# Causal masks added by VectorE and a two-part values operand in the last two batches of an attention and mixer kernel

## Chip, cores and metric

One NeuronCore of a Trainium2 chip. The metric is the device time of one execution in microseconds (us); the kernel before took 888.46 us (median of 3 runs, 887.33 to 892.19). All data are float32.

## What is computed

The kernel chains three layers over 4 batches of 448 rows and 768 channels. The change lies in the first, causal attention with 12 heads of 64 channels:

```python
scores = scale * np.matmul(q, k.transpose(0, 1, 3, 2))
mask = np.triu(np.ones((seq, seq), dtype=bool), k=1)
scores = np.where(mask, -1000000000.0, scores)
scores = scores - np.max(scores, axis=-1, keepdims=True)
attn = np.exp(scores)
attn = attn / (np.sum(attn, axis=-1, keepdims=True) + 1e-09)
return np.matmul(attn, v)
```

A token and channel mixer follows (`u = x + (relu(xt @ w_tok1) @ w_tok2)` transposed back, then `u + relu(u @ w_ch1) @ w_ch2`), and a gated layer with a spatial product and an output projection.

## The kernel before

**Tiling.** Two heads are a pair; there are 6 pairs a batch and 24 in all, numbered n = 0 to 23. A pair's 448 queries are four chunks, `CHUNKS` (line 25): number 0 has 64 queries, 1, 2 and 3 have 128 each. Chunk i sees only the keys up to its own end, so it is 64, 192, 320 or 448 columns wide; j is the head within the pair.

**Two ways to multiply.** Pairs 0 to 11 (the first two batches, `whole`, line 279) give float32 operands to TensorE as they are. Pairs 12 to 23 split each operand into a high part that float32r holds and the low rest, and use three products of parts (high by high, high by low, low by high). From pair 12 on a pair has only one buffer of each kind (`side`, `before`, lines 160 to 166).

**A pair's steps** (`pair_jobs`, line 275):
- `lq`, `lv`: loads of queries, keys and values on the SP queue; `qs` scales the queries on GpSimd (POOL). For pairs 12 to 23 `qh`, `ql`, `kl`, `vh`, `vl` make the parts, on ScalarE (ACT) and POOL.
- `SA`, `SB` (line 334): the scores of chunks 3 and 0, and of 2 and 1, on TensorE (PE). Behind each chunk's products (line 351) come matmuls that add the mask: a selecting matrix `eye` by a triangle `tri` of -1e9 (line 359), two of them for chunk 0 and four for each other chunk, so 14 a pair.
- `M` (line 371): VectorE (DVE) finds the negated maximum of both heads of a chunk at once, out of PSUM. `E` (line 378): ACT takes the exponential out of PSUM into the tiles `pbig` and `psml` and accumulates the sums. `R` (line 382): DVE inverts the sums. `Pn` (line 393): POOL multiplies the eight exponentials of a pair by them.
- `T0`, `Ta`, `Tb` (line 402): PE transposes the blocks; ACT copies them out (`H`), and for pairs 12 to 23 DVE makes the low parts (`L`).
- `PV0`, `PVa`, `PVb` (lines 435 to 463): PE multiplies values by transposed blocks into one PSUM bank (`v`), one head in the upper and one in the lower 64 rows. For pairs 12 to 23 each product is three matmuls (lines 440 to 442), 21 a pair.
- `UE`: ACT copies the result into `U`. `UT`, `XH`, `XL`: PE turns it back, ACT and DVE make parts for the token mixer.

**The rest in the same list.** `group_jobs` does the token mixer after every third pair. `weight_jobs` changes 24 channel-mixer weights from pairs of words to float32 in three DVE steps (lines 104, 106, 108) and two POOL steps (lines 71, 77), and stores them to DRAM. `channel_jobs` loads them again (`wb`) for each batch and does the channel mixer: 24 blocks of 18 matmuls a batch (lines 119 to 121, tile `cps`). The last layer stands behind the list, written in order.

**The order.** All these steps are jobs with an engine, a planned cost, predecessors, a rank and perhaps a PSUM bank or buffer. `emit` (line 214) takes, again and again, the ready job that can start earliest by its plan, and of several the one of lowest rank; ranks are the pair or block number plus an offset from the table `RK` (line 260). That fixes the order of each engine's instructions; an engine whose next instruction isn't ready waits, whatever stands behind it. Pairs 12 to 23 are thus mixed with the channel mixer of earlier batches, which fills PE.

## Time and profile before

| what | value |
|---|---|
| median of 3 runs | 888.46 us |
| profiled execution, its own time | 889.3 us |
| its span, first to last instruction | 887.5 us |
| busy: PE, DVE, ACT, POOL | 854.4, 432.8, 300.3, 293.5 us |
| mean granted TensorE clock | 0.988 of full speed |
| matmuls | 4768 |

A busy time is the sum over which an engine had at least one instruction running. Matmuls are pipelined: one row of PE overlaps the next, so what a matmul costs is the distance from its start to the next start, not its own duration. An engine's idle time before an instruction is put down to what released it.

### The profile page before, as it was taken

Reading aid. Unit: us, or ns where it says so; the run is one execution under the profiler, and the core shown is the slowest. Engines: PE = TensorE matmul, PEld = TensorE weight load, DVE = VectorE, ACT = ScalarE, POOL = GpSimd, SP = SyncE. Lnnn points to the kernel's source line nnn. Section 1 sums busy time; section 2 is a strip of 40 time slices with the busy share of each in tenths; the row PEclk is TensorE's granted clock in tenths of the full one; section 3 lists DMA queues with packets and bytes.
Section 4 is the critical chain, followed back from the end, with each engine's and each line's share of the span. In section 5 each row is a group of like instructions: output and inputs, shape, how many; then the busy total and the mean of one; then the engine's idle time right before and its main releaser. Section 6 shows DMA issues by size and latency. Waiting matters only on the chain.

```text
span 887.5 us, 12703 instructions
## 1 busy us (share of the span) xinstructions
PE 854.4 (96%) x4768; PEld 740.2 (83%) x4768; DVE 432.8 (49%) x775; ACT 300.3 (34%) x816; POOL 293.5 (33%) x378
## 2 busy tenths in 40 slices
PE   7898998788999999999999999999999999999998
PEld 5576766677789899998988899999999888889997
DVE  4795886885634533433443345511134543467441
ACT  5765564242223423333342301200013431433110
POOL 3588697774633223323233201200003200224000
PEclk9999999898999999999999999999999999999999
DMA  4676685876762555455344538876662200000112
GB/s 142 188 265 219 215 302 201 308 258 276 272 251 87 195 178 205 140 176 198 114 161 155 175 107 285 318 259 216 213 215 78 71 1 1 1 1 31 70 56 94
DMA packets 45613, 148.65 MB, mean 167 GB/s; under 512 B 17008, under 2 KB 21744, under 8 KB 45552
## 3 DMA queue, kind: packets, MB, share of 16 engines
q1 hardware_dynamic: 42096, 128.96, 43.0%
q10 hardware_dynamic: 3456, 18.88, 5.4%
q8 instruction: 38, 0.62, 0.3%
q14 instruction: 23, 0.19, 0.1%
HBM read 123.44 MB, written 24.38 MB: 167 GB/s over the span
## 4 chain that ended last, share of the span: by engine, by line
PE 83%; POOL 6%; DVE 4%; DMA 3%; ACT 2%; issue 2%; ACTq 0%; POOLq 0%; SPq 0%
PE cps L119 13%; PE cps L120 12%; PE cps L121 12%; PE pst L406 4%; PE sa L351 3%; PE pso L437 3%; PE psg L120 2%; PE psg L121 2%; PE psg L119 2%; PE pso L121 2%; PE pso L119 2%; PE pso L120 2%; PE psv L119 2%; PE psv L120 2%; PE psv L121 2%; POOL pbig L393 2%
## 5 line engine op out<-in xcount | busy, mean ns | idle before, releaser
L119 PE MATMUL cps<-uhl,wb 128*128 128x448 f32 x288 | 109.3, 380 | 3.8 <-DMA wb<-w 3.8
L119 PE MATMUL cps<-hid,wb 128*128 128x448 f32 x288 | 108.3, 376 | 2.3 <-DMA wb<-w 1.4
L120 PE MATMUL cps<-uhl,wb 128*128 128x448 f32 x288 | 106.3, 369 | 0.0
L121 PE MATMUL cps<-uhl,wb 128*128 128x448 f32 x288 | 106.1, 368 | 0.0
L121 PE MATMUL cps<-hid,wb 128*128 128x448 f32 x288 | 105.4, 366 | 0.0
L120 PE MATMUL cps<-hid,wb 128*128 128x448 f32 x288 | 105.3, 365 | 0.0
L393 POOL TENSOR_SCALAR pbig<-pbig,rcp 128x448 f32<-128x448 f32 (+1 forms) x96 | 65.1, 687 | 90.6 <-DVE rcp L384 85.3
L84 DVE SCALAR_TENSOR_TENSOR hid<-cps,hid 128x448 fp32r<-128x448 f32 x48 | 29.9, 623 | 108.8 <-ACT hid L702 108.8
L378 ACT ACTIVATE pbig<-sa,nm 128x448 f32<-128x448 f32 (+1 forms) x72 | 42.6, 597 | 105.4 <-DVE nm L371 59.6
L702 ACT ACTIVATE hid<-cps 128x448 fp32r<-128x448 f32 x48 | 26.1, 544 | 139.9 <-PE cps L121 139.9
L710 DVE TENSOR_TENSOR U<-cps,U 128x448 f32<-128x448 f32 x48 | 29.9, 624 | 81.4 <-PE cps L121 80.6
L77 POOL TENSOR_TENSOR winl<-win,winh 128x1536 fp32r<-128x1536 f32 x4 | 14.8, 3691 | 165.1 <-ACT winh L69 165.1
L371 DVE TENSOR_REDUCE nm<-sa 128x2 f32<-128x896 f32 (+1 forms) x72 | 46.2, 680 | 39.0 <-PE sa L359 38.6
L119 PEld LDWEIGHTS cps<-uhl,wb 128*128 128x128 f32 x288 | 54.8, 190 | 8.5 <-issue 4.1
L119 PEld LDWEIGHTS cps<-hid,wb 128*128 128x128 f32 x288 | 54.1, 188 | 8.0 <-DVE U L710 2.3
L121 PEld LDWEIGHTS cps<-uhl,wb 128*128 128x128 f32 x288 | 54.8, 190 | 4.6
L120 PEld LDWEIGHTS cps<-uhl,wb 128*128 128x128 f32 x288 | 55.0, 191 | 4.0
L121 PEld LDWEIGHTS cps<-hid,wb 128*128 128x128 f32 x288 | 54.1, 188 | 4.6
L120 PEld LDWEIGHTS cps<-hid,wb 128*128 128x128 f32 x288 | 54.2, 188 | 4.1
L406 PE MATMUL pst<-ident,pbig 128*128 128x128 f32 x288 | 48.3, 279 | 8.4 <-POOL pbig L393 8.2
L77 POOL TENSOR_TENSOR wn<-wn 128x768 fp32r<-128x768 f32 x24 | 46.3, 1928 | 1.6
L406 PEld LDWEIGHTS pst<-ident,pbig 128*128 128x128 f32 x288 | 35.0, 142 | 12.7 <-POOL pbig L393 11.2
(186 smaller groups left out, 1974.1 us busy)
## 6 DMA issues: line engine op xcount, KB each, us to landing
wb<-w SPq DMA_DIRECT2D x96, 768.0 KB, 4.3
dbl<-in_w SPq DMA_DIRECT2D x24, 768.0 KB, 5.7
w<-wn ACTq DMA_DIRECT2D x24, 768.0 KB, 5.3
stage<-in_qkv SPq DMA_DIRECT2D x24, 448.0 KB, 4.3
out_t<-out SPq DMA_DIRECT2D x24, 224.0 KB, 1.9
dbl<-in_winu SPq DMA_DIRECT2D x4, 768.0 KB, 5.8
dbl<-in_winv SPq DMA_DIRECT2D x4, 768.0 KB, 6.0
dbl<-in_wout SPq DMA_DIRECT2D x4, 768.0 KB, 4.3
```

The source lines that it names most:

```text
L77: e.tensor_tensor(lo, x, hi.bitcast(F32), op=ALU.subtract)
L84: nc.vector.scalar_tensor_tensor(lo, x, 0.0, hi.bitcast(F32), op0=ALU.max, op1=ALU.subtract)
L119: nc.tensor.matmul(ps, ah, bh, start=(first and i == 0), stop=False)
L120: nc.tensor.matmul(ps, ah, bl, start=False, stop=False)
L121: nc.tensor.matmul(ps, al, bh, start=False, stop=(last and i == n - 1))
L351: nc.tensor.matmul(out, x[rows, q0:q1], y[rows, S : 2 * S][:, ks[j]], start=(t == 0), stop=False, skip_group_check=True)
L371: nc.vector.tensor_reduce(nm[:M], S_.ps[:M, :, o : o + W], axis=mybir.AxisListType.X, op=ALU.max, negate=True)
L378: nc.scalar.activation(P(n, i)[:M, j, :], S_.ps[:M, j, o : o + W], AF.Exp, bias=SM[n, i][:M, j : j + 1], scale=1.0, accum_out=sums[n % 2][ ...
L393: nc.gpsimd.tensor_scalar(x, x, rcp[n % 2][:M, 2 * ((i - 1) % 4) + j :][:, 0:1], 1.0, op0=ALU.mult, op1=ALU.mult)
L406: nc.tensor.transpose(me.ps[:, o : o + M], src(), ident[:M, :M])
L437: nc.tensor.matmul(out, v32[e][:, k], m[0], start=first, stop=last, skip_group_check=True)
L710: nc.vector.tensor_tensor(U[b][:, d, :], first.ps, U[b][:, d, :], op=ALU.add)
```

## The change

- For pairs 12 to 23 the mask matmuls go. `make_mask` writes two mask tiles once, on POOL, before pair 12. In place of one maximum for both heads, `M` becomes one DVE instruction for each chunk and head, eight a pair: it adds the mask to the scores in PSUM, writes the negated sum into the exponential's own tile in SBUF, and keeps the least element, the negated maximum. `E` reads that tile in SBUF with scale -1 and no longer holds the PSUM bank.
- For pairs 12 to 23 the values' high and low parts stand side by side in one stationary operand of 128 columns for each chunk and head. Each product is two matmuls (by the high and the low part of the transposed block), so the product of the two low parts is included too. The two heads can't share a bank's rows now: each head has its own chain `PV0`, `PVa`, `PVb`, one after the other in the one bank `v`, 16 matmuls a pair. ACT copies one half of the rows into `U` and DVE adds the other half, for each head.
- Values of these pairs are loaded by one DMA instead of three; their parts are made by six POOL instructions instead of four.
- For pairs 0 to 11 the multiplication `Pn` of the narrow chunks 0 and 1 (four a pair) moves from POOL to ACT.
- The planned costs of several jobs, `NARROW` and nearly all offsets in `RK` change, and with them the order of instructions on all engines.

```diff
-NARROW = (980, 1150, 1160)
+NARROW = (840, 1300, 1280)
...
-                v = slot("G7", [2, VS], F32R, "v")
-                parts12[what] = [v[:, 0, :], v[:, 1, :]]
-                for t in parts12[what]:
-                    nc.gpsimd.memset(gaps(t).bitcast(F32), 0.0)
+                v = parts12[what] = slot("G7", [8, 2 * D], F32R, "v")
+                nc.gpsimd.memset(v[64:128, 0, :].bitcast(F32), 0.0)
+                nc.gpsimd.memset(v[0:64, 7, :].bitcast(F32), 0.0)
...
-    RK = dict(s=53.0, q=-0.3, v=14.0, e=26.8, pn=-68.2, f=43.8, hl=-6.2, pv=-11.9, ue=33.0, ut=-111.3, x=-99.8, h=59.1, hr=-23.0, u=59.0, uc=55.2, us=45.6, ld=-58.4, ch=71.8, hd=-31.0, ad=-6.0, nw=76.8, nh=72.7, wi=295.1)
+    RK = dict(s=74.7, q=-0.5, v=28.2, e=26.7, pn=-105.7, f=41.2, hl=-38.3, pv=-27.5, ue=29.5, ut=-154.8, x=-87.8, h=60.5, hr=-82.0, u=81.8, uc=64.9, us=61.3, ld=-6.8, ch=79.3, hd=-95.7, ad=-78.8, nw=69.0, nh=16.7, wi=310.3)
...
+        places = [(slice(0, 128), slice(1, 7), slice(1, 7)), (slice(0, 64), slice(0, 1), slice(0, 1)), (slice(64, 128), slice(0, 1), slice(7, 8))]
...
+        def make_mask(_):
+            masks12.extend(slot(tag, [S], F32, "mask") for tag in ("mask", "p1"))
+            for t, o in zip(masks12, (0, S - 128)):
+                nc.gpsimd.memset(t, 0.0)
+                diag = t[:, o : o + 128]
+                nc.gpsimd.affine_select(out=diag, in_=diag, compare_op=ALU.is_ge, fill=MASKED, base=0, pattern=[[-1, 128]], channel_multiplier=1)
+
+        if n == 2 * NP:
+            job(("mk",), "POOL", 1200, make_mask, after=[("T0", n - 1), ("Ta", n - 1, 0), ("Ta", n - 1, 1), ("SA", n - 1), ("SB", n - 1)], rank=r + RK["q"])
...
-                            nc.tensor.matmul(out, x[rows, q0:q1], y[rows, S : 2 * S][:, ks[j]], start=(t == 0), stop=False, skip_group_check=True)
+                            nc.tensor.matmul(out, x[rows, q0:q1], y[rows, S : 2 * S][:, ks[j]], start=(t == 0), stop=(t == 2), skip_group_check=True)
+                    if not whole:
+                        continue
...
+                    nc.vector.tensor_tensor_reduce(
+                        out=P(n, i)[:M, j, :],
+                        in0=S_.ps[:M, j, o : o + W],
+                        in1=masks12[0][:M, :W] if j == 0 or M == 64 else masks12[1][:M, S - W : S],
+                        scale=-1.0,
+                        scalar=3.0e38,
+                        op0=ALU.add,
+                        op1=ALU.min,
+                        accum_out=SM[n, i][:M, j : j + 1],
+                    )
...
+                    src = S_.ps[:M, j, o : o + W] if whole else P(n, i)[:M, j, :]
+                    nc.scalar.activation(P(n, i)[:M, j, :], src, AF.Exp, bias=SM[n, i][:M, j : j + 1], scale=1.0 if whole else -1.0, accum_out=acc)
...
+                    top_ = job(("M", n, i, j), "DVE", 150 + W / 0.96, low, after=[S_, *old, ("mk",)], rank=r + RK["e"]).uses(S_)
...
+                if whole and i < 2:
+                    nc.scalar.mul(x, x, f)
+                else:
+                    nc.gpsimd.tensor_scalar(x, x, f, 1.0, op0=ALU.mult, op1=ALU.mult)
...
+        def pvx_parts(j, V, blocks, dst, last):
+            def run(_):
+                for c, o in blocks:
+                    s0 = CHUNKS[c][0]
+                    for k in range(2):
+                        nc.tensor.matmul(V.ps[:, s0:S], split_tiles("v")[:, c + 3 * j], dst[k][:, o : o + S - s0], start=False, stop=(last and k == 1 and c == 3), skip_group_check=True)
...
+                W_ = job(("PV0", n), "PE", 420, pv0_parts(j), after=[("L", "T0", n), vfit] + [("PV0", n)] * j, rank=r + RK["pv"], bank="v")
...
+                def first_part(_, j=j, x=x, W_=W_):
+                    nc.scalar.copy(x, W_.ps[64 - 64 * j : 128 - 64 * j, :S])
+
+                def both_parts(_, j=j, x=x, W_=W_):
+                    nc.vector.tensor_tensor(x, W_.ps[64 * j : 64 * j + 64, :S], x, op=ALU.add)
```

## Rows read from the trace of the kernel before

**Rows 1.** Stretches of the span: each engine's busy us (instructions), granted clock, DMA share, GB/s.

```profile
0.00:153.50 153.50, 137.88 (x850) 98.26 (x851) 107.53 (x174) 90.47 (x297) 107.08 (x151) 0.98 0.67 221
153.50:245.50 92.00, 79.71 (x456) 66.77 (x454) 65.59 (x85) 28.80 (x85) 59.49 (x64) 0.93 0.76 274
245.50:515.00 269.50, 267.77 (x1683) 241.27 (x1684) 104.10 (x196) 96.80 (x275) 81.72 (x140) 1.00 0.49 167
515.00:700.00 185.00, 185.00 (x906) 169.55 (x905) 67.58 (x131) 33.54 (x59) 21.73 (x10) 1.00 0.61 210
```

**Rows 2.** Waits of PE in its first 250 us: us in total, times, longest.

```profile
PE pst L406 <- POOL pbig L393: 7.0, 7, 2.2
...
PE cps L119 <- DMA wb<-w: 5.1, 3, 3.8
```

**Rows 3.** Timeline of PE, mask matmuls (L359): start us, us, instruction.

```profile
382.99 0.33 PE L359 MATMUL sa<-cst 64*128 64x128 f32 x4
383.24 0.47 PE L119 MATMUL cps<-hid,wb 128*128 128x448 f32 x1
...
404.18 0.31 PE L359 MATMUL sa<-cst 64*128 64x128 f32 x4
404.32 0.34 PE L351 MATMUL sa<-qk 64*64 64x64 f32 x6
404.49 0.23 PE L359 MATMUL sa<-cst 64*64 64x64 f32 x2
404.65 0.47 PE L119 MATMUL cps<-hid,wb 128*128 128x448 f32 x1
```

**Rows 4.** Timeline of PE, values by transposed blocks of one pair.

```profile
395.12 0.36 PE L440 MATMUL pso<-T,v 128*128 128x448 f32 x1
...
395.73 0.34 PE L440 MATMUL pso<-Tab,v 128*64 128x384 f32 x1
...
396.26 0.28 PE L440 MATMUL pso<-Tab,v 128*64 128x256 f32 x1
...
396.61 0.22 PE L440 MATMUL pso<-Tab,v 128*64 128x128 f32 x1
...
396.79 0.39 PE L440 MATMUL pso<-Tab,v 128*128 128x384 f32 x1
...
397.77 0.27 PE L441 MATMUL pso<-Tab,v 128*128 128x128 f32 x1
397.88 0.27 PE L442 MATMUL pso<-Tab,v 128*128 128x128 f32 x1
398.00 0.42 PE L119 MATMUL cps<-hid,wb 128*128 128x448 f32 x1
398.25 0.36 PE L120 MATMUL cps<-hid,wb 128*128 128x448 f32 x1
```

**Rows 5.** Groups by line and shape on DVE and ACT: busy us, mean ns.

```profile
L710 DVE TENSOR_TENSOR U<-cps,U 128x448 f32<-128x448 f32 x48 | 29.9, 624 | 81.4 <-PE cps L121 80.6
...
L371 DVE TENSOR_REDUCE nm<-sa 128x2 f32<-128x896 f32 x24 | 26.0, 1083 | 24.1 <-PE sa L359 24.1
...
L378 ACT ACTIVATION_READ_ACCUMULATOR pbig<-sa,nm 128x1 f32 x72 | 14.3, 199 | 0.0
...
L464 ACT COPY U<-pso 128x448 f32<-128x448 f32 x24 | 12.8, 532 | 33.7 <-PE pso L442 26.1 <-PE pso L437 7.6
```

**Rows 6.** Groups on POOL, the multiplications Pn: wide chunks together, then narrow ones.

```profile
L393 POOL TENSOR_SCALAR pbig<-pbig,rcp 128x448 f32<-128x448 f32 (+1 forms) x96 | 65.1, 687 | 90.6 <-DVE rcp L384 85.3
...
L393 POOL TENSOR_SCALAR psml<-psml,rcp 128x192 f32<-128x192 f32 x48 | 24.7, 524 | 0.0
...
L393 POOL TENSOR_SCALAR psml<-psml,rcp 64x64 f32<-64x64 f32 x48 | 16.7, 360 | 0.0
```

**Rows 7.** Timeline of DVE, one step of the weights' change of format, twice.

```profile
143.19 0.55 DVE L104 TENSOR_SCALAR wn<-dbl 128x768 uint32<-128x768 uint32 x1
...
154.71 2.50 DVE L104 TENSOR_SCALAR wn<-dbl 128x768 uint32<-128x768 uint32 x1
```

More of the change, by code (lines that the diff above doesn't have):

```diff
@@ L435, in product @@
         def product(out, k, m, first=False, last=False):
[L436 to L442 removed]
+            nc.tensor.matmul(out, v32[e][:, k], m[0], start=first, stop=last, skip_group_check=True)
         def pv0(me):
@@ L458, in pvx, with pv0_parts, run @@
             return run
-        last = V
-        for j in range(2):
-            last = job(("PVa", n, j), "PE", 650 if whole else 3 * 174, pvx(j, [(1, 0)], da[j], False), after=[last, ("L", "Ta", n, j)], rank=r + RK["pv"]).uses(V)
-            last = job(("PVb", n, j), "PE", 680 if whole else 3 * (117 + 59 + 51 * j), pvx(j, [(2, 0), (3, 256)], db[j], j == 1), after=[last, ("L", "Tb", n, j)], rank=r + RK["pv"]).uses(V)
-        UE = job(("UE", n), "ACT", 540, lambda _: nc.scalar.copy(U[b][:, p, :], V.ps[:, :S]), after=[last], rank=r + RK["ue"]).uses(V)
+        def pv0_parts(j):
+            def run(me):
+                me.ps = psa.tile([128, 512], F32, tag=me.tile, name="pso")
+                for k in range(2):
+                    nc.tensor.matmul(me.ps[:, :S], split_tiles("v")[:, 7 * j], d0[k], start=(k == 0), stop=False, skip_group_check=True)
+            return run
```

94 lines of the change are left out of this document (56 added, 38 removed).

## The prediction

> **What bounds the kernel now.** First the table of stretches [rows 1], which divides the span by what TensorE (PE) waits for. From 245.5 to 515 us PE has an instruction running for 267.77 of 269.50 us, and from 515 to 700 us for all of 185.00; every other engine is below half of either stretch. There only less work for PE can shorten the kernel, and any such work counts in full. Ahead of that PE is idle for 15.6 us until 153.5 us and for 12.3 us until 245.5 us; in the second of these the mean granted clock is 0.93, so part of it ran at 1.2 GHz in place of 2.4. VectorE (DVE) and GpSimd (POOL) are at 71% and 65% there, ScalarE (ACT) at 31%. Then the waits of PE in its first 250 us [rows 2]: the longest sum, 7.0 us, is for POOL's multiplication of the exponentials, the next, 5.1 us, for channel weights that come back from DRAM. So this early part is bound by chains through all engines, not by one of them.
>
> Then the timeline of PE inside the dense part [rows 3, 4]. Matmuls overlap, so I read costs as distances between starts. The scores of pairs 12, 13 and 14 fall into the loose stretch up to 245.5 us, those of pairs 15 to 23 into the dense one.
>
> **Masks leave PE.** The four mask matmuls behind chunk 3 take 404.18 to 404.32, so 0.14 us; those behind chunk 2 sit in the same way between two score products, another 0.14; the two behind chunk 0 take 404.49 to 404.65, 0.16; the four behind chunk 1 take 382.99 to 383.24, 0.25 [rows 3]. Together 0.69 us a pair. The last two numbers contain the step from the half-height matmuls to the full-height ones of the channel mixer, which stays when the scores themselves come last. If all of that stays, only 0.28 us goes; if none, 0.69. I take 0.50, in the middle: two matmuls of 64 columns and four of 64 to 128 must be worth something. Over 12 pairs 6.0 us, bounds 3.4 and 8.3.
>
> The Trainium skill, TensorEngine Tiling (Array Packing), Key Properties, speaks against the middle value: a change of tiling mode (not of the tile) drains TensorE. By that rule the step out of a score block is a drain that stays, the gain is the 3.4 us of the lower bound, and the time below would be 881.6 in place of 879.0. The trace agrees so far that the step out takes 0.16 and 0.25 where a step inside takes 0.14; how much of it is the masks' own it doesn't show.
>
> **Values by blocks: 21 matmuls become 16.** The block of one pair runs from 395.12 to 398.00, 2.88 us [rows 4]. From starts three matmuls apart: 448 columns cost (395.73 - 395.12) / 3 = 0.203 us, 384 cost 0.177, 256 cost 0.117, 128 cost 0.06 behind a stationary operand of 64 columns and 0.11 behind one of 128 (397.77 to 397.88). Afterwards every operand has 128 columns, and for each head there are two of each width: 4 x (0.203 + 0.177 + 0.117 + 0.11) = 2.43 us, 0.45 less. The block now comes in two pieces, and leaving one costs 0.25 in place of 0.20 (398.00 to 398.25), so 0.40 a pair, 4.8 us in all. If the narrow ones stay at 0.06 it is 0.60 a pair, 7.2 us.
>
> **What takes the masks over.** DVE loses four maxima a pair, of both heads and 2048 columns together, and gains eight additions with a maximum over the same 2048 columns, plus two additions of 448 columns. The old maxima cost 1.083 us for 896 columns, so 2.5 us a pair; the nearest row for the new ones reads PSUM and SBUF and writes SBUF, 624 ns for 448 columns [rows 5]. Eight at that price would be 5.0 us, the same rate as the maxima 2.5; six of eight are narrower, so I take 3.2. With 2 x 0.624 for the second halves DVE has about 1.9 us more a pair, bounds 1.2 and 3.7. ACT gets one more copy, 0.532 us [rows 5]. In the dense part both are hidden: DVE is busy for 104.10 and ACT for 96.80 of 269.50 us [rows 1], and PE has channel blocks that need neither. If that cover went, the nine dense pairs would cost 9 x 1.9 = 17 us.
>
> In the loose stretch the cover is thin. DVE is busy for 65.59 of 92.00 us with the weights' change of format that PE waits for. Three pairs bring 5.7 us there; I let half reach PE, 2.8 us, bounds 0 and 5.7. The mask tiles cost POOL four instructions once; at 687 ns, the row of its wide multiplications [rows 6], at most 2.7 us. Pair 12's maxima now stand behind them and behind pair 11's transposes, and what is queued behind those maxima on DVE waits too: the format steps. I price it at nothing, since POOL and DVE have slack of 32.5 and 26.4 us in that stretch, and keep 2.7 as the bound.
>
> The Trainium skill, VectorE: DVE Perf Modes, Two Vector instructions with no wait between them, adds a price: an operation that also writes out its accumulator is two instructions. No row of before has one on DVE. ACT's separate read of an accumulator takes 199 ns [rows 5]; eight of that size would be an estimated 1.6 us a pair, or 4.8 us more for the three loose pairs, and with half of it on the path the time below would be 881.4.
>
> **The narrow multiplications.** In pairs 0 to 11 four of eight move from POOL to ACT. A pair's eight now cost POOL 4 x 0.687 + 2 x 0.524 + 2 x 0.360 = 4.5 us, of which 1.77 us move, 39% [rows 6]. Of PE's 7.0 us behind this line [rows 2] I count 39%, 2.7 us, as gained, bounds 0 and 7.0. ACT has room: 90.47 of 153.50 us [rows 1] and 12 x 1.77 = 21 us more at POOL's own prices.
>
> **Edits at no cost.** One load in place of three on the SP queue: fewer issues of the same bytes. The values' six part-making instructions in place of four on POOL: each extra one is at most the 0.360 us of a 64 x 64 multiplication [rows 6], and POOL is at 81.72 of 269.50 us. The exponential from SBUF: same columns. New ranks and planned costs: they move no work between engines; in the dense part any order that keeps PE supplied takes the same time, in the loose part it can go either way, which I put into the range with 5 us on both sides.
>
> **The sum.** Masks 6.0 and values 4.8 give 10.8 us less PE work. A quarter of it, 2.7 us, belongs to pairs 12 to 14 in the loose stretch; half of that is lost to waiting, leaving 9.4. The early gain of 2.7 and the early loss of 2.8 cancel. The profiled execution took 889.3 us, so 879.9; the median of the runs is 0.84 lower, so 879.0 us.
>
> **Rivals.**
> - *Early stretch tightens.* All 10.8 us count, 2.7 us of waits for POOL go, and half of the slow clock's price: 0.07 of 92 us is 6.4 us, so 3.2. That is 16.7 us, 871.8. For it: one format step on DVE takes 0.55 us with POOL idle and 2.50 us while POOL works [rows 7], so 21 us taken from POOL can speed DVE too. With the masks at their upper bound it reaches 869. Against it: the waits for channel weights stay.
> - *Early stretch eats the gain.* All 5.7 us of DVE work and the 2.7 us of mask tiles reach PE in place of the 2.8 I counted: 884.6. For it: the second stretch is already DVE's.
> - *Slower: the second head waits for the one bank.* Head 1's first product can start only when ACT (0.532 us) and DVE (0.624 us) [rows 5] have emptied head 0's bank. If the fixed order puts too little PE work between, PE stands for 1.16 us and everything behind it too: 12 x 1.16 = 13.9 us, 892.9. It loses more than the change gains from 0.8 us a pair on (9.4 / 12). Against it: the plan counts 540 and 620 for these two steps and so places other blocks between; for it: it doesn't know what else waits in ACT's and DVE's queues.
> - *The masks cost nothing where they are:* the 3.4 us above, 881.6, inside the forecast's own range.
>
> **How the numbers follow.** A measurement here tells about 0.5% (4.4 us) from no change, so faster means below 884.0 and slower above 892.9. The forecast has 0.58 (872 to 884), the tighter early stretch 0.16, the eaten gain 0.15, the waiting second head 0.11. Faster is 0.58 + 0.16 = 0.74, same 0.15, slower 0.11. The range takes in the upper bounds of masks and values with the tight early stretch, 867, and the eaten gain with 4 us of worse order, 889.
>
> **What would show it.** Right: no L359 behind pair 11, blocks of values near 2.4 us in two pieces, PE busy throughout from 250 us to the end, and a span about 10 us shorter, all of it by 515 us. Wrong: PE waits that name ACT or DVE ahead of the second head's first product; PE idle until 245 us up by more than 5 us behind format steps or weights; the new DVE instructions beyond 0.8 us at 448 columns.

## The result and the profile after

The changed kernel takes 867.72 us (median of 4 runs, 866.49 to 868.02) beside 888.39 us for the kernel before on the same chip: ratio 0.9757, 95% interval 0.9727 to 0.9788, or 20.7 us less. The forecast was 9.5 us less, so the sign is right and the size is less than half of what came. The time lies in the range, near the rival in which the early stretch tightens (871.8).

| profiled execution | before | after |
|---|---|---|
| span | 887.5 us | 866.2 us |
| PE busy, matmuls | 854.4 us, 4768 | 835.9 us, 4540 |
| span without PE | 33.1 us | 30.3 us |
| DVE, ACT, POOL busy | 432.8, 300.3, 293.5 us | 451.1, 324.4, 284.2 us |
| mean granted clock | 0.988 | 0.988 |

So 18.5 of the 21.3 us of span are PE's busy time and 2.8 are idle time. PE's work was to fall by 10.8 us by the forecast; the first question is where the other 8 came from.

The same stretches as in [rows 1], of the kernel after (columns: PE, PEld, DVE, ACT, POOL busy us and instructions, granted clock, DMA share, GB/s):

```profile
0.00:153.50 153.50, 134.70 (x851) 95.91 (x852) 123.17 (x183) 103.38 (x345) 102.26 (x111) 0.97 0.77 256
153.50:245.50 92.00, 84.20 (x435) 73.10 (x434) 52.80 (x101) 26.90 (x72) 49.15 (x61) 0.93 0.72 259
245.50:515.00 269.50, 269.50 (x1574) 242.97 (x1573) 122.05 (x339) 107.65 (x296) 87.63 (x162) 1.00 0.51 173
515.00:700.00 185.00, 185.00 (x909) 168.55 (x908) 73.09 (x154) 41.28 (x75) 23.02 (x11) 1.00 0.53 180
```

Against [rows 1], the dense stretch has lost its last 1.7 us of idle PE, although DVE has 18 us and ACT 11 us more to do in it: the cover that the forecast named holds. From 515 to 700 us PE is busy throughout, as before. The first stretch is worse, 18.8 us of idle PE for 15.6. The second is better, 7.8 for 12.3, and DVE has 12.8 us and POOL 10.3 us less to do there; part of that work has moved ahead of 153.5 us (DVE has 15.6 us more there). The granted clock in the second is 0.93 as before. The two early stretches together give 1.3 us of idle time only.

PE's timeline after, in the dense part: two score blocks of one pair and the two value blocks of another (start us, us, instruction; L360 scores, L500 and L509 values, L119 to L121 channel mixer):

```profile
386.68 1.02 PE L360 MATMUL sa<-qk 64*128 64x448 f32 x12
387.63 0.47 PE L119 MATMUL cps<-uhl,wb 128*128 128x448 f32 x1
387.94 0.37 PE L120 MATMUL cps<-uhl,wb 128*128 128x448 f32 x1
...
391.18 0.36 PE L121 MATMUL cps<-uhl,wb 128*128 128x448 f32 x1
391.47 1.02 PE L360 MATMUL sa<-qk 64*128 64x320 f32 x12
392.42 0.47 PE L119 MATMUL cps<-uhl,wb 128*128 128x448 f32 x1
...
405.49 0.56 PE L500 MATMUL pso<-T,v 128*128 128x448 f32 x2
405.89 0.93 PE L509 MATMUL pso<-Tab,v 128*128 128x384 f32 x6
406.65 0.42 PE L119 MATMUL cps<-hid,wb 128*128 128x448 f32 x1
406.91 0.36 PE L120 MATMUL cps<-hid,wb 128*128 128x448 f32 x1
...
409.15 0.57 PE L500 MATMUL pso<-T,v 128*128 128x448 f32 x2
409.55 0.92 PE L509 MATMUL pso<-Tab,v 128*128 128x384 f32 x6
410.31 0.41 PE L119 MATMUL cps<-hid,wb 128*128 128x448 f32 x1
```

The two blocks of before, with their masks, start here (their ends are the channel matmuls at 383.24 and 404.65 in [rows 3]):

```profile
381.90 0.71 PE L351 MATMUL sa<-qk 64*128 64x320 f32 x6
...
403.17 0.37 PE L121 MATMUL cps<-hid,wb 128*128 128x448 f32 x1
403.47 0.88 PE L351 MATMUL sa<-qk 64*128 64x448 f32 x6
...
404.96 0.36 PE L120 MATMUL cps<-hid,wb 128*128 128x448 f32 x1
```

A score block is 0.95 us both times (386.68 to 387.63, 391.47 to 392.42). The two of before took 1.18 us (403.47 to 404.65) and 1.34 us (381.90 to 383.24). So the masks were worth 2.52 - 1.90 = 0.62 us a pair. A head's values take 1.16 us (405.49 to 406.65, and 409.15 to 410.31), two heads 2.32 in place of 2.88 [rows 4]. Leaving a value block still costs 0.05 us over a usual step of 0.20 (406.65 to 406.91), now twice a pair. That is 0.51 us a pair. Over 12 pairs: 7.4 us from masks and 6.1 us from values, 13.5 together. The other pairs agree with this one: summed from start to start over the twelve, scores and masks take 23.0 us for 30.6, and the values 28.0 for 34.7, before the 0.6 us of the added leaving steps.

The waits of PE in its first 250 us, after (us in total, times, longest):

```profile
PE sb L360 <- ACT psml L407: 4.1, 2, 3.6
PE cps L119 <- DMA wb<-w: 3.9, 2, 2.2
...
PE pst L446 <- POOL pbig L432: 1.7, 4, 0.6
```

The wait for POOL's multiplication, 7.0 us in [rows 2], is 1.7 us, a gain of 5.3. A new one stands in its place, 4.1 us of scores behind ACT's exponentials (L407). It is not the price of the multiplications that moved to ACT: with them back on POOL (relief out, below) it is 3.1 us. The wait for weights is 3.9 us for 5.1.

DVE and ACT groups by line and shape, after (busy us, mean ns; L394 mask and maximum, L531 and L528 the two halves of values, L407 exponential, L430 ACT's multiplication):

```profile
L531 DVE TENSOR_TENSOR U<-pso,U 64x448 f32<-64x448 f32 x24 | 14.9, 622 | 33.8 <-ACT U L528 33.7
L394 DVE CUSTOM_DVE_ANT_0 pbig<-sa,mask 128x448 f32<-128x448 f32 x24 | 13.9, 618 | 0.2 <-PE sa L360 0.2
L528 ACT COPY U<-pso 64x448 f32<-64x448 f32 x24 | 12.7, 528 | 43.8 <-PE pso L509 43.8
L394 DVE CUSTOM_DVE_ANT_0 pbig<-sa,mask 128x320 f32<-128x320 f32 x24 | 10.8, 488 | 12.5 <-PE sa L360 12.5
L430 ACT ACTIVATE psml<-psml,rcp 128x192 f32<-128x192 f32 x24 | 9.4, 441 | 0.0
L394 DVE CUSTOM_DVE_ANT_0 psml<-sa,mask 128x192 f32<-128x192 f32 x24 | 7.8, 353 | 0.0
L394 DVE DVE_READ_ACCUMULATOR2_ANT nm<- 128x1 f32 x72 | 6.0, 83 | 0.0
```

The added DVE work is as forecast: a pair has two each of 618, 488, 353 and (64 columns) 210 ns, 3.3 us for the 3.2 assumed, and with 2 x 0.62 us for the second halves and less 2.7 us of old maxima (1.083, 0.822, 0.548 and 0.271 us by width in the trace of before) it has 1.9 us more, as forecast, though the forecast took 2.5 us for the old maxima. ACT's copy of one half takes 528 ns, and its multiplication of 192 columns 441 ns where POOL's took 524 [rows 6].

### The profile page after: what moved, and what is told of

Read it like the earlier page. It is cut to its first block, busy times and chain, and to the rows that moved or that the text cites. A ratio compares the mean times of both kernels' runs of the same rounds, so it can differ in the third digit from the quotient of the medians.

```text
span 866.2 us, 12334 instructions
## 1 busy us (share of the span) xinstructions
PE 835.9 (97%) x4540; PEld 726.0 (84%) x4540; DVE 451.1 (52%) x943; ACT 324.4 (37%) x876; POOL 284.2 (33%) x358
## 4 chain that ended last, share of the span: by engine, by line
PE 85%; POOL 6%; DVE 3%; DMA 3%; ACT 1%; issue 1%; ACTq 0%; SPq 0%; POOLq 0%
PE cps L119 14%; PE cps L120 13%; PE cps L121 13%; PE pst L446 4%; PE sa L360 3%; PE pso L476 3%; PE psg L120 2%; PE psg L121 2%; PE pso L121 2%; PE psg L119 2%; PE pso L119 2%; PE pso L120 2%; PE psv L119 2%; PE psv L120 2%; PE psv L121 2%; PE pso L509 2%
## 5 line engine op out<-in xcount | busy, mean ns | idle before, releaser
L119 PE MATMUL cps<-hid,wb 128*128 128x448 f32 x288 | 108.9, 378 | 3.9 <-DMA wb<-w 3.9
L119 PE MATMUL cps<-uhl,wb 128*128 128x448 f32 x288 | 109.1, 379 | 1.9 <-ACT uhl L69 1.9
L121 PE MATMUL cps<-hid,wb 128*128 128x448 f32 x288 | 106.0, 368 | 0.0
L121 PE MATMUL cps<-uhl,wb 128*128 128x448 f32 x288 | 105.8, 367 | 0.0
L119 PEld LDWEIGHTS cps<-hid,wb 128*128 128x128 f32 x288 | 54.6, 189 | 9.4 <-DMA wb<-w 2.6
L119 PEld LDWEIGHTS cps<-uhl,wb 128*128 128x128 f32 x288 | 54.6, 190 | 7.0 <-ACT uhl L69 2.3
L77 POOL TENSOR_TENSOR winl<-win,winh 128x1536 fp32r<-128x1536 f32 x4 | 14.8, 3698 | 135.1 <-ACT winh L69 135.1
L121 PEld LDWEIGHTS cps<-uhl,wb 128*128 128x128 f32 x288 | 54.7, 190 | 4.5
L121 PEld LDWEIGHTS cps<-hid,wb 128*128 128x128 f32 x288 | 54.5, 189 | 4.6
L71 POOL TENSOR_SCALAR v<-stage 64x64 fp32r<-64x64 f32 (+1 forms) x36 | 13.0, 372 | 110.4 <-PE pso L509 109.4
L77 POOL TENSOR_TENSOR wn<-wn 128x768 fp32r<-128x768 f32 x24 | 48.5, 2021 | 1.8
L446 PE MATMUL pst<-ident,pbig 128*128 128x128 f32 x288 | 46.3, 278 | 2.0 <-POOL pbig L432 1.7
L407 ACT ACTIVATE pbig<-pbig,nm 128x448 f32<-128x448 f32 (+1 forms) x48 | 29.2, 610 | 45.5 <-DVE nm L394 40.5
```

The lines of the kernel that those rows point to most:

```text
L77: e.tensor_tensor(lo, x, hi.bitcast(F32), op=ALU.subtract)
L119: nc.tensor.matmul(ps, ah, bh, start=(first and i == 0), stop=False)
L121: nc.tensor.matmul(ps, al, bh, start=False, stop=(last and i == n - 1))
L407: nc.scalar.activation(P(n, i)[:M, j, :], src, AF.Exp, bias=SM[n, i][:M, j : j + 1], scale=1.0 if whole else -1.0, accum_out=acc)
L446: nc.tensor.transpose(me.ps[:, o : o + M], src(), ident[:M, :M])
```

## Experiments

All ratios are to the kernel before on the same chip, with a 95% interval. Four parts of the change are told apart: **masks** (on DVE), **values** (two parts side by side), **relief** (ACT multiplies narrow chunks in place of POOL), and **order** (`RK`, `NARROW` and planned costs).

### One part taken out of the changed kernel

**Order out.**

```diff
-NARROW = (840, 1300, 1280)
+NARROW = (980, 1150, 1160)
-    RK = dict(s=74.7, q=-0.5, v=28.2, e=26.7, pn=-105.7, f=41.2, hl=-38.3, pv=-27.5, ...
+    RK = dict(s=53.0, q=-0.3, v=14.0, e=26.8, pn=-68.2, f=43.8, hl=-6.2, pv=-11.9, ...
...
-        A = job(("SA", n), "PE", 1520 if whole else 1070, score([(3, 0), (0, S)]), after=fit, rank=r + RK["s"], bank="sa")
+        A = job(("SA", n), "PE", 1350 if whole else 1070, score([(3, 0), (0, S)]), after=fit, rank=r + RK["s"], bank="sa")
...
```

The other planned costs of whole pairs (`SB`, `R`, `Pn`, `PV0`, `PVa`, `PVb`) go back in the same way.

> All three changes of work, but with the ranks, the weights' planned costs and the planned costs of unchanged jobs as they were before. Theory A (the 7 us beyond PE's smaller work come from the new order in the first 250 us): about 874.7 us, PE idle in the first 250 us back at 30 us or more. Theory B (they come from the narrow multiplications that leave POOL): about 868 us, as the changed kernel.

Measured 874.93 us, 0.9835 (0.9806 to 0.9864). That is 14.0 us less than before, near the 13.5 us that the blocks gave up; but the relief is still in this kernel, with a share that it doesn't tell. Some 7 us of the result are gone with the order. PE's idle time in the first 250 us is 31.1 us here and 26.6 us in the changed kernel.

**Relief out.**

```diff
-                if whole and i < 2:
-                    nc.scalar.mul(x, x, f)
-                else:
+                if True:
...
-            eng, c = ("ACT", 230 + q1) if whole and i < 2 else ("POOL", 400 + q1 * 0.9 - 100 * (not whole))
+            eng, c = ("POOL", (350 if whole and i < 2 else 400 - 100 * (not whole)) + q1 * 0.9)
```

> The changed kernel with all eight multiplications of pairs 0 to 11 on POOL again. Theory A: within 2 us of 867.7. Theory B: about 875 us, with the longest wait of PE in the first 250 us again for POOL's multiplication (7 us).

Measured 885.55 us (10 runs, 881.72 to 889.85), 0.9956 (0.9932 to 0.9980): 18 us of the 20.7 are gone, where 0 and 7 us were expected. The forecast's term for the relief was 2.7 us, with a bound of 7.0.

**Masks out** (back on PE):

```diff
...
-            ... start=(t == 0), stop=(t == 2), skip_group_check=True)
-                    if not whole:
-                        continue
+            ... start=(t == 0), stop=False, skip_group_check=True)
...
-                if whole:
-                    top_ = J["M", n, i]
-                else:
-                    top_ = job(("M", n, i, j), "DVE", 150 + W / 0.96, low, ...
+                top_ = J["M", n, i]
```

> The changed kernel with the mask matmuls and the maxima of before in pairs 12 to 23. Both theories: masks are worth 0.62 us a pair on PE (1.90 us of scores a pair after, 2.52 before), so 867.7 + 7.5 = 875.2 us. If the step from half-height to full-height matmuls were all that the last masks cost, 871.

Measured 872.98 us, 0.9807 (0.9774 to 0.9840): 5.3 us lost by the medians, 4.4 by the ratios, against 7.4 us of PE work by the timeline.

**Values out** (three products into one bank, as before):

```diff
-    nc.tensor.matmul(me.ps[:, :S], split_tiles("v")[:, 7 * j], d0[k], ...
...
-    nc.tensor.matmul(V.ps[:, s0:S], split_tiles("v")[:, c + 3 * j], dst[k][:, o : o + S - s0], ...
...
+    nc.tensor.matmul(out, vh[:, k], m[0], start=first, stop=False, skip_group_check=True)
+    nc.tensor.matmul(out, vh[:, k], m[1], start=False, stop=False, skip_group_check=True)
+    nc.tensor.matmul(out, vl[:, k], m[0], start=False, stop=last, skip_group_check=True)
```

> The changed kernel with three products of parts for values by blocks, one bank for both heads. Both theories: 2.87 us a pair in place of 2.33, so 867.7 + 6.5 = 874.2 us. If the second head's wait for the one bank costs anything in the changed kernel, less than that.

Measured 872.12 us, 0.9806 (0.9777 to 0.9835): 4.4 us lost, against 6.1 us of PE work. Both fall a little short; taking out a part also shifts the early order, but that this is why isn't shown. With intervals of some 3 us on either side of each ratio the counted sizes are not excluded.

### One part alone, put into the kernel before

**Values alone.**

```diff
-            nc.tensor.matmul(out, vh[:, k], m[0], start=first, stop=False, skip_group_check=True)
-            nc.tensor.matmul(out, vh[:, k], m[1], start=False, stop=False, skip_group_check=True)
-            nc.tensor.matmul(out, vl[:, k], m[0], start=False, stop=last, skip_group_check=True)
...
+                    nc.tensor.matmul(me.ps[:, :S], split_tiles("v")[:, 7 * j], d0[k], start=(k == 0), stop=False, skip_group_check=True)
...
```

> The kernel before with the two-part values alone, old order. Theory A (PE's smaller work passes to the end in full, the early stretch goes by order and GpSimd relief together): 12 x 0.54 = 6.5 us less than before, about 882.4. Theory C (part of the gain in each edit is given back in the early stretch under the old order): 884 to 886.

Measured 881.74 us (10 runs), 0.9911 (0.9871 to 0.9951).

**Masks alone.**

```diff
-            job(("M", n, i), "DVE", c, top, after=[S_], rank=r + RK["e"]).uses(S_)
...
+                    top_ = job(("M", n, i, j), "DVE", 150 + W / 0.96, low, after=[S_, *old, ("mk",)], rank=r + RK["e"]).uses(S_)
```

> The kernel before with the masks by VectorE alone, old order. Theory A: 12 x 0.62 = 7.5 us less, about 881.4. Theory C: 884 to 887, because VectorE's extra work delays the weights' format steps in the first 250 us.

Measured 882.49 us, 0.9885 (0.9828 to 0.9943). Each alone gains 8 to 10 us, with an interval that holds its counted size (6.1 and 7.4 us).

**Relief alone.**

```diff
-                nc.gpsimd.tensor_scalar(x, x, rcp[n % 2]..., 1.0, op0=ALU.mult, op1=ALU.mult)
+                if whole and i < 2:
+                    nc.scalar.mul(x, x, f)
+                else:
+                    nc.gpsimd.tensor_scalar(x, x, f, 1.0, op0=ALU.mult, op1=ALU.mult)
```

> The kernel before with the narrow multiplications of pairs 0 to 11 on ScalarE alone, old order. Theory A: the relief needs the new order, so within 2 us of before, as the kernel with all parts and the old order lost exactly the early gain. Theory B (relief of GpSimd alone shortens the early stretch): 4 us or more faster than before.

Measured 899.95 us (10 runs), 1.0095 (1.0057 to 1.0132): slower by 10 us, which was not foreseen. Its stretches:

```profile
0.00:153.50 153.50, 135.96 (x852) 97.57 (x853) 105.43 (x167) 104.64 (x346) 80.55 (x103) 1.00 0.63 209
153.50:245.50 92.00, 73.52 (x402) 61.92 (x401) 67.62 (x90) 28.93 (x84) 57.77 (x61) 0.85 0.75 269
```

POOL falls from 107.08 us to 80.55 us in the first stretch, so the relief is there. But the second stretch has 18.5 us of idle PE and a granted clock of 0.85, while DVE and POOL there have as much to do as before [rows 1]: the work on the weights was not drawn forward into the room that POOL had got (the last weight's last POOL step starts at 242.7 us, for 238.9 before).

**Order alone.**

```diff
-NARROW = (980, 1150, 1160)
+NARROW = (840, 1300, 1280)
-    RK = dict(s=53.0, ..., nw=76.8, nh=72.7, wi=295.1)
+    RK = dict(s=74.7, ..., nw=69.0, nh=16.7, wi=310.3)
```

> The kernel before with the new ranks and planned costs alone. Theory A, as the changed kernel without the relief lost 18 us: slower than before by about 5 to 11 us, the loss all in the first 250 us. Theory D (the new order is better by itself): about 881.

Measured 902.79 us, 1.0119 (1.0046 to 1.0192): slower by 12.6 us by the medians, 4 to 17 by the interval. Its stretch up to 250 us:

```profile
0.00:250.00 250.00, 210.51 (x1224) 154.75 (x1225) 184.29 (x250) 116.56 (x366) 174.10 (x210) 0.94 0.69 236
```

and the timeline of DVE and POOL around pairs 10 and 11 (L104 one format step, L430 multiplications, L71 and L77 parts):

```profile
155.84 0.81 POOL L430 TENSOR_SCALAR psml<-psml,rcp 128x192 f32<-128x192 f32 x2
155.92 5.91 DVE L104 TENSOR_SCALAR wn<-dbl 128x768 uint32<-128x768 uint32 x1 [1.54 <-POOL pbig L430]
156.63 1.80 POOL L77 TENSOR_TENSOR wn<-wn 128x768 fp32r<-128x768 f32 x1
...
158.40 2.21 POOL L77 TENSOR_TENSOR qk<-stage,qk 128x448 fp32r<-128x448 f32 x2
160.60 0.82 POOL L71 TENSOR_SCALAR wn<-wn 128x768 fp32r<-128x768 f32 x1
161.50 1.99 POOL L77 TENSOR_TENSOR wn<-wn 128x768 fp32r<-128x768 f32 x1
```

PE stands for 39.5 us, for 28.4 in the kernel before. POOL is busy for 174.10 of 250 us, hardly more than before (168.44), so its load is not what differs; the weights' steps (L71, L77 on `wn`) now stand between the pairs' multiplications. One format step on DVE, which takes 0.55 us with POOL idle [rows 7], takes 5.91 us here: it begins at 155.92 and ends at 161.83, while POOL goes from one instruction to the next; its first pause, 0.08 us, is at 161.42. PE's longest sum of waits is for DVE's low parts (`xs`), 7.1 us.

### Do relief and order need each other?

Relief alone loses 10 us, order alone 13 us, and yet the whole change gains more than its smaller PE work. The theory (A in the expectation): each needs the other.

**Relief and order together**, masks and values as before:

```diff
+NARROW = (840, 1300, 1280)
+    RK = dict(s=74.7, ..., nw=69.0, nh=16.7, wi=310.3)
+                if whole and i < 2:
+                    nc.scalar.mul(x, x, f)
```

> The kernel before with the relief of GpSimd and the new ranks and planned costs together, masks and values as before. Alone the relief cost about 10 us and the order about 13. Theory A (each needs the other): about 7 us faster than before, 881 to 883, the first channel block near 174 us in place of 187. Theory E (the losses add, and what saves the changed kernel lies in masks or values): 900 us or more.

Measured 877.78 us, 0.9876 (0.9850 to 0.9901): 11.8 us faster, where the two losses would add up to 22 us slower. So the theory holds for these two parts, and by more than was expected. PE's idle time up to 250 us is 22.5 us, for 36.7 with the relief alone and 39.5 with the order alone.

**Relief with the two weight ranks only** (`nw`, `nh`; the other offsets as before):

```diff
-    RK = dict(..., nw=76.8, nh=72.7, wi=295.1)
+    RK = dict(..., nw=69.0, nh=16.7, wi=295.1)
```

> The relief of GpSimd with the old order except for two offsets: those of the weights' format steps on VectorE and GpSimd (nw and nh) are the new ones. Theory A1 (what the new order does with the relief is to give GpSimd's time to the weights): at least 10 us faster than the relief alone, 890 or less, with the last weight done by about 215 us in place of 243. Theory A2 (the offsets work only all together): within 3 us of the relief alone, near 900.

Measured 887.84 us (10 runs), 0.9975 (0.9952 to 0.9998): 11 to 12 us better than the relief alone. There the room is used: the last weight's last POOL step starts at 205 us in place of 243. So the relief alone was slow through late weights, as far as this one run tells.

**The second head at once** (planned costs of the two steps that empty the bank set to nothing, so that the list may put the second head earlier):

```diff
-                c_ = job(("UE", n, j), "ACT", 540, first_part, ...
-                done.append(job(("UF", n, j), "DVE", 620, both_parts, ...
+                c_ = job(("UE", n, j), "ACT", 0, first_part, ...
+                done.append(job(("UF", n, j), "DVE", 0, both_parts, ...
```

> The changed kernel, with the planned costs of the two steps that empty the first head's bank set to 0, so that the list puts the second head's products about 0.3 us behind the first's. My slower rival: PE stands for some 0.9 us in each of 12 pairs, 11 us more than the changed kernel, about 878, with waits of PE that name ScalarE or VectorE before the second head. If PE finds the bank free all the same: 868.

Measured 866.93 us, 0.9742 (0.9711 to 0.9773), as the changed kernel. The second head's block now starts 2.60 us after the first (3.66 in the changed kernel), and PE waits for nothing between 245 and 520 us.

**More relief** (chunk 2 to ACT as well):

```diff
-                if whole and i < 2:
+                if (whole and i < 3):
...
-            eng, c = ("ACT", 230 + q1) if whole and i < 2 else ...
+            eng, c = ("ACT", 300 + q1) if (whole and i < 3) else ...
```

> The changed kernel with the multiplications of chunk 2 moved to ScalarE too in pairs 0 to 11 (six of eight there, planned at 300 ns and 1 ns a column). If GpSimd still bounds the early stretch: 2 to 5 us faster than 867.7. If ScalarE, at 103 of the first 153.5 us, is now as close to the limit: the same or slower.

Measured 882.57 us, 0.9921 (0.9902 to 0.9941): 15 us worse than the changed kernel. Pair 11's sums are inverted only at 170 us (143.7 in the changed kernel). PE's waits up to 300 us name ACT's multiplications with 5.1 us, where POOL's took 1.7, and DVE's low parts with 5.5. That ACT alone makes the chain late isn't shown: in the first 153.5 us it is busy for 100.21 us, for 103.38 in the changed kernel.

### Is it the weights, or what stands ahead of the first channel block?

**Old weight ranks in the changed kernel, and in the kernel with the new order alone.** The theory tried (A1): the two weight ranks decide, for the gain of the changed kernel and for the loss of the order alone.

```diff
-    RK = dict(..., nw=69.0, nh=16.7, wi=310.3)
+    RK = dict(..., nw=76.8, nh=72.7, wi=310.3)
```

> The changed kernel with the old offsets nw and nh for the weights' format steps alone. Theory A1 (the gain of the early stretch is GpSimd's time given to the weights): loses the early gain, 874 to 878, the last weight at 230 us or later in place of 210. Otherwise within 2 us of 867.7.

> The new order without relief, masks and values as before, but with the old nw and nh. Theory A1 (without the relief the weights' steps take GpSimd's time from the pairs, which come late): most of the 13 us loss goes, 888 to 893, and the first channel block is back from 210 us to about 190. Otherwise near 902.

Measured 869.20 us, 0.9783 (0.9738 to 0.9828), though the last weight is late; and 909.71 us, 1.0248 (1.0208 to 1.0287), worse still than the order alone. Both go against the theory, so it falls: the changed kernel's last weight may come 77 us later (its last POOL step starts at 287 us for 210) at no price beyond the interval, and the order alone is not slow because of its early weights.

**The second head closer still** (planned costs -220 and -160 for head 0):

```diff
-                c_ = job(("UE", n, j), "ACT", 540, first_part, ...
-                done.append(job(("UF", n, j), "DVE", 620, both_parts, ...
+                c_ = job(("UE", n, j), "ACT", 540 if j else -220, first_part, ...
+                done.append(job(("UF", n, j), "DVE", 620 if j else -160, both_parts, ...
```

> The changed kernel with the second head's products of pairs 12 to 23 directly behind the first head's, by planned costs of -220 and -160 ns for the two steps that empty the first head's bank; the two or three channel matmul groups that stood between come later. My slower rival's price: 1.16 us and the hand-overs, 1.2 to 1.5 us a pair, so 882 to 886, with waits of PE that name VectorE before the second head's first product.

Measured 868.29 us, 0.9774 (0.9740 to 0.9807). Its timeline around one pair's heads:

```profile
405.30 0.42 PE L119 MATMUL cps<-hid,wb 128*128 128x448 f32 x1
...
405.50 0.53 ACT L528 COPY U<-pso 64x448 f32<-64x448 f32 x1 [2.97 <-PE pso L509]
...
406.06 0.62 DVE L531 TENSOR_TENSOR U<-pso,U 64x448 f32<-64x448 f32 x1 [2.80 <-ACT U L528]
...
406.73 0.30 PEld L500 LDWEIGHTS pso<-T,v 128*128 128x128 f32 x2 [0.38 <-DVE U L531]
406.73 0.67 PE L500 MATMUL pso<-T,v 128*128 128x448 f32 x2
```

The bank is free at 406.68, 1.4 us behind the end of the first head's block at 405.30. Six channel matmuls stand in that time. What PE loses is two long steps, 0.37 us into the second head's block (406.37 to 406.73) and 0.31 behind its first product (406.73 to 407.04), in place of 0.20 each: 0.28 us a pair. The distance of the heads is 2.60 us, the same as with planned costs of nothing, so this run brings them no closer. Two heads with nothing between them were not to be had from the list; what that would cost was not tried.

**Relief for all pairs**, the dense ones too:

```diff
-                if whole and i < 2:
+                if i < 2:
```

> The changed kernel with the narrow multiplications of pairs 12 to 23 on ScalarE too. In the dense part neither engine bounds anything, so only pairs 12 to 14 count: within 3 us of 867.7, if the order stays about as good.

Measured 866.70 us, 0.9753 (0.9718 to 0.9788), no different: in the dense part POOL is not what PE waits for.

**What the times follow.** The channel mixer is PE's filler: ahead of its first block PE has nothing but the pairs' chains and the token mixer's. That block waits for the token mixer's group 3, which waits for pairs 9 to 11 turned back. The channel matmuls as a group by tile (times in ns least, median and most; first and last start in us), of the kernel before:

```profile
L119 PE MATMUL cps<-uhl,wb x36: 358/369/712, 187.2 to 221.2; 128*128 128x448 f32 x36
```

The same group of the changed kernel:

```profile
L119 PE MATMUL cps<-uhl,wb x36: 358/368/722, 174.3 to 206.0; 128*128 128x448 f32 x36
```

The first block starts 12.9 us earlier. Over the profiled executions that have the PE work of one or of the other:

| PE work of before (first five), then of after | first channel block | profiled time |
|---|---|---|
| relief and order together | 175.6 us | 876.2 us |
| before | 187.2 | 889.3 |
| order alone | 209.6 | 903.3 |
| order alone, old weight ranks | 217.1 | 909.4 |
| before, weights held (below) | 181.0 | 880.4 |
| after | 174.3 | 868.0 |
| order out | 179.9 | 874.3 |
| relief out | 199.0 | 881.7 |
| chunk 2 to ACT too | 204.5 | 882.6 |
| after, old weight ranks | 172.6 | 865.0 |
| second head at once | 173.1 | 866.3 |
| second head closer still | 173.5 | 867.9 |
| after, weights held (below) | 166.9 | 861.8 |

Within each half the time rises with that start: from the earliest to the latest, 0.80 us for 1 us in the first half and 0.55 in the second. Three do not fit: the relief alone (186.2 us, yet 899.2), whose first block comes as early as before but whose next ones are far apart; the relief with two weight ranks (192.7, 889.4); and the relief for all pairs (178.5, 866.4).

Why the start is late in the kernel before, DVE's timeline tells:

```profile
163.13 2.46 DVE L106 SCALAR_TENSOR_TENSOR wn<-dbl,wn 128x768 uint32<-128x768 uint32 x1
...
166.58 2.43 DVE L108 SCALAR_TENSOR_TENSOR wn<-dbl,wn 128x768 uint32<-128x768 uint32 x1
169.04 0.87 DVE L77 TENSOR_TENSOR xs<-psn,xs 64x128 fp32r<-64x128 f32 x2
```

Pair 11's low parts (L77, at 169.04) are the last thing that the token group waits for, and they stand behind format steps that take 2.4 us each while POOL makes weight parts. Pair 11 was turned back at 162.2. In the changed kernel:

```profile
160.65 0.62 DVE L394 CUSTOM_DVE_ANT_0 pbig<-sa,mask 128x448 f32<-128x448 f32 x1 [0.21 <-PE sa L360]
161.20 0.08 DVE L394 DVE_READ_ACCUMULATOR2_ANT nm<- 128x1 f32 x1
161.20 0.62 DVE L394 CUSTOM_DVE_ANT_0 pbig<-sa,mask 128x448 f32<-128x448 f32 x1
...
162.00 0.85 DVE L77 TENSOR_TENSOR xs<-psn,xs 64x128 fp32r<-64x128 f32 x2
```

Turned back at 160.6, low parts at 162.00: 1.4 us in place of 6.8. So 7.0 of the 12.9 us arise here. Of the rest, 2.2 lie in the group's first products, 6.2 us long before (169.38 to 175.59, with a granted clock of 0.50 up to 174.3) and 4.0 after (163.56 to 167.52); what stands behind them was not followed. This theory (F in the expectations) says: hold back the weights that nobody needs yet until the token group is through, and either kernel becomes faster.

**Weights held, in the kernel before and in the changed one:**

```diff
+        for w in W0[15:]:
+            w.after.append(J["u", 3, 2])
```

`W0` lists the first format step of each of the 24 weights; in the changed kernel it is `W0[17:]`; `("u", 3, 2)` is the last product of token group 3, the fourth.

> The kernel before, in which the format steps of weights 15 to 23 wait for the last product of the fourth token group (pairs 9 to 11). Theory F (the chain from pair 11 to the first channel block bounds the early stretch, and DVE's format steps stand in its way): first channel block near 178 us in place of 187, 5 to 9 us faster than before, 880 to 884, though the last weight comes 20 us later. Theory G (the weights bound it): slower than before by 5 us or more.

> The changed kernel with weights 17 to 23 held back in the same way. Theory F: its chain is already 12 us shorter than before's and loses at most 2 or 3 us more, 865 to 868. Theory G: slower by 5 us or more.

The kernel before: 885.07 us (10 runs), 0.9954 (0.9926 to 0.9982), 4.9 us faster, first channel block at 181.0 for 187.2. The changed kernel: 861.53 us (861.00 to 867.87), 0.9705 (0.9662 to 0.9749), first block at 166.9 for 174.3. Its stretches:

```profile
0.00:153.50 153.50, 139.39 (x868) 98.83 (x869) 118.49 (x181) 103.90 (x347) 103.90 (x120) 0.99 0.77 260
153.50:245.50 92.00, 83.80 (x453) 74.03 (x452) 54.88 (x111) 26.98 (x71) 43.77 (x53) 0.96 0.69 251
```

and its DVE timeline at the same point:

```profile
155.45 0.62 DVE L394 CUSTOM_DVE_ANT_0 pbig<-sa,mask 128x448 f32<-128x448 f32 x1 [3.24 <-PE sa L360]
...
156.80 0.86 DVE L77 TENSOR_TENSOR xs<-psn,xs 64x128 fp32r<-64x128 f32 x2
```

DVE now waits 3.24 us for PE ahead of that point in place of standing in format steps, the granted clock in the second stretch is 0.96 for 0.93, and PE's idle time up to 250 us is 22.3 us for 26.6. One dependency moved the first block in both kernels and the time with it, by 5 and 6 us at the medians, though the last weight came later (last POOL step at 254.8 us for 238.9, and 243.6 for 210.2). In the kernel before the interval excludes no change, so there it is shown that what stands ahead of the first block counts. In the changed kernel the two intervals overlap (0.9662 to 0.9749, 0.9727 to 0.9788), so its 6 us are likely and not shown. The theory's sizes were off: it gained a little less than forecast before and more after.

## Why the prediction was right or wrong

**Right: the dense part.** PE was its bound and is never idle there after the change, and DVE and ACT did their added work beside it. That the work taken from PE counts in full fits the runs: masks alone and values alone gain what was counted, within their intervals.

**Wrong in size: masks.** Counted at 0.50 us a pair between 0.28 and 0.69, measured 0.62: 7.4 us for 6.0. The middle value failed because a full step is not kept when the scores come last: 18 score and mask products of chunks 3 and 0 took 1.18 us, the 12 that stay take 0.95, and 20 became 12 at 0.95 for 1.34.

The forecast weighed the Trainium skill there (TensorEngine Tiling (Array Packing), Key Properties: a change of tiling mode drains TensorE) as a reason for the lower bound, 3.4 us. The block lengths do not bear that out as a price that stays in the block: 0.62 of the 0.69 us went. The steps at its two ends are long in both kernels. Behind the first channel matmul it is 0.31 us (387.63 to 387.94 after, 404.65 to 404.96 before), but behind transposes in full tiles it is 0.29 too (402.64 to 402.93 after). Into a score block it is 0.29 after (391.18 to 391.47) and 0.30 before (403.17 to 403.47), where into a value block in full tiles it is 0.21 (405.28 to 405.49). So if a drain is there, these rows have it ahead of the block, with about 0.1 us, and never among the 0.69.

**Wrong in size: values.** Counted at 0.40 us a pair with a bound of 0.60, measured 0.51: 6.1 us for 4.8. The failed step is the 0.11 us for each 128-column matmul behind a stationary operand of 128 columns. Six matmuls behind the first two take 0.76 us (405.89 to 406.65); less 2 x 0.177 and 2 x 0.117 that leaves 0.17 for two, so 0.06 for one and 0.11 for the other. The trace of before had that pattern [rows 4]: 0.06 from the first narrow matmul behind a wider one (397.71, L440) to the next (397.77, L441), and 0.11 from there on. After the change the narrow ones come in twos, so half of their steps are of the cheap kind; the forecast took the dear one for all four.

**Not shown: half of the loose pairs' gain lost.** The kernel with the order out gains 14.0 us, more than the whole 13.5, but it has the relief too, and its interval is 2.6 us wide on either side. So no run tells whether the 1.35 us taken off for pairs 12 to 14 were lost.

**Wrong in kind: "The early gain of 2.7 and the early loss of 2.8 cancel", and ranks worth 5 us at most.** This is the step that failed most: of the 11.2 us between the 9.5 forecast and the 20.7 measured, the blocks have 2.7, and some 7 go with the order. The relief was sized as a share of one wait of PE, and the order at nothing beside it. In fact taking the relief out of the changed kernel costs 18 us, putting it alone into the kernel before costs 10, the new order alone costs 13, and both together gain 12. What goes with these times, in most of the kernels, is when the channel mixer can begin, and so how long PE has only the early chains to run. That it is the cause is shown for the 5 us of the held weights in the kernel before and argued for the rest. For the relief alone it fails: that kernel begins its first block as early as before (186.2 us for 187.2) and yet loses 10 us. The forecast read [rows 2] as a list of separate waits; it did not ask which job opens the filler work, nor follow the chain of pair 11 on DVE, although [rows 7] shows the 2.50 us step that stands in it.

The page accounts for it so: PE busy fell by 18.5 us, of which 13.5 are masks and values, and idle time by 2.8. The other 5 us of busy time lie mostly in early work that did not change: from start to start the scores and masks of whole pairs and the first products of the token mixer (`psh`) sum up to 71.0 us, for 76.9 before. Part of that is the clock: before, 10 us of this work fell into stretches with a granted clock of 0.50, the 1.2 GHz level, and after the change 3. But other work fell into them instead. PE is busy for 17.15 us at that level before (75.4 to 78.8, 136.8 to 140.2, 167.5 to 174.3 and 208.5 to 215.3 us) and for 17.96 after (128.4 to 135.2, 152.2 to 155.6, 176.1 to 182.9 and 217.1 to 220.5). So less time at the low level is not where the 5 us came from, and their cause stays open.

**The rivals.** *Early stretch tightens* was the nearest, and its sign for POOL was right: the wait for POOL fell by 5.3 us, for the 7.0 that it took away whole. But the granted clock of the second stretch is 0.93 as before, so the 3.2 us that it took for a faster clock did not come in that row. *Early stretch eats the gain* did not come: DVE has 52.80 us there, for 65.59. *The second head waits for the one bank* was not met: even where the list was pushed to put the heads together, it kept six channel matmuls between them and PE lost 0.28 us a pair, 3.3 in all, which the times (866.93 and 868.29 us) don't show; that the price is 1.16 us with nothing between was not tested. *The masks cost nothing* is refuted by the blocks.

**Terms costed at nothing.** The mask tiles took POOL 2.4 us (154.29 to 156.75, four instructions), within the bound of 2.7. The accumulator read of the new DVE instruction is there, as a second instruction of 83 ns, and its row at 161.20 starts together with the next maximum: it costs no time of its own.

The Trainium skill (VectorE: DVE Perf Modes, Two Vector instructions with no wait between them) says that such an operation is two instructions, and the trace agrees. The estimate of 1.6 us a pair drawn from ACT's read, with 881.4 us for the whole, was wrong.

**Open.** Masks and values together, without relief and order, were not run. Relief and order gain 11.8 us without masks and values, whose blocks give up 13.5 us, and all together gain 20.7, not 25: why the two don't add up was not settled. Which of the 23 offsets shorten pair 11's chain was not tried one by one. That late weights make the relief alone sparse behind its first block rests on one run with two ranks changed, and in the changed kernel later weights cost nothing beyond the interval.

## What to carry to other kernels

In a kernel whose order comes from a list, ask first which job opens the work that keeps the bound engine busy, and follow the chain to it on every engine: here 1 us of later start went with 0.55 to 0.80 us of time in most kernels, and no list of waits shows it. Cost new ranks and a moved step together and give them a range from experiments, not a few us: here each alone lost 10 us and both gained 12. Work taken from the engine that is the bound counted in full here as far as the intervals tell, and distances between starts give its size block by block, the long step behind a block included where the number of blocks changes.

## What was not expected of the hardware

- **A DVE step beside POOL.** The same format step, 128x768 words, SBUF to SBUF, took 0.55 us and 2.50 us [rows 7] and 5.91 us in the kernel with the order alone, where POOL had instruction behind instruction. The Trainium skill (SBUF — State Buffer, Who interferes with whom) says that a DVE instruction that uses the port pair shared with POOL and one of POOL's exclude each other for a whole instruction. The two-input steps of 2.43 and 2.46 us (L108, L106) agree with one POOL instruction of 1.8 to 2.0 us waited out. The 2.50 and 5.91 us rows are longer than any single POOL instruction beside them (0.98 and 1.80 us), so there DVE would have waited out several. Less work on POOL did not shorten these steps by itself: with the relief alone POOL is busy for 141.38 of the first 250 us, for 168.44 before, and the weights' 72 format steps on DVE take 84.9 us, for 82.6.
- **An addition with a maximum on DVE** out of PSUM and SBUF into SBUF runs at the price of a plain addition of two tensors: 618 ns for 448 columns, beside 622 ns for L531.
- **A 128-column matmul** by a stationary operand of 128 columns takes 0.06 us from start to start as the first behind a wider one and 0.11 behind that, in [rows 4] and, by the sum of two, after the change; by operands of 64 columns all three take 0.06 (396.61 to 396.79). Each matmul has a weight load of its own (4540 of each), whose starts are 0.11 us apart in that row of 128-column operands. Whether that or the operand shared by the first two makes the difference wasn't told apart.
